# Linear attention with a gated FFN: o transposed tile by tile, output projection among the last Q groups, phi of Q on VectorE

## The chip, the core and the metric

The kernel runs on one core of a Trainium2 chip. The core has five engines, each with an instruction queue of its own that it works off in order: PE (TensorE, matrix products into PSUM), DVE (VectorE), ACT (ScalarE), POOL (GpSimd) and SP (SyncE, which only starts transfers). Sixteen DMA engines carry the transfers between HBM and SBUF. The metric is the device time of one execution in microseconds (us), the median of several runs.

## What is computed

Inputs are bf16: x is 2048 tokens of 1024, wqkv 1024 x 3072, wo 1024 x 1024, the FFN's weights 1024 x 3584 (gate, up) and 3584 x 1024 (down). The reference, cut to what matters:

```python
x = A_x
xn = _layernorm(x, axis=-1)
# _A_ref: 32 heads of 32
phi = lambda t: jnp.where(t > 0, t + 1, jnp.exp(t)) + 1e-6
pq, pk = phi(q), phi(k)
kv = jnp.einsum("bhsd,bhse->bhde", pk, v)
z = jnp.einsum("bhsd->bhd", pk)
num = jnp.einsum("bhqd,bhde->bhqe", pq, kv)
den = jnp.einsum("bhqd,bhd->bhq", pq, z)[..., None] + 1e-6
o = num / den
s = o @ wo                               # [2048, 1024]
# _B_ref
f = (_silu(xn @ w_gate) * (xn @ w_up)) @ w_down
return x + s * _silu(f)
```

## The kernel before

It has three stages. The first (lines 256 to 597) normalizes x, transposes it, computes K and V for 16 tiles of 128 tokens, and accumulates the sums of pk times v (kvz). It also computes the Q groups of tokens 0 to 1023 (pass 0). The second (lines 599 to 705) is where the change lies. The third is the FFN with the final sum.

Products with seven instead of eight blocks are used for Q and for the FFN. A Q group (class QGroup, line 205) is 256 columns of Q for 1024 tokens: seven products of four matmuls each (M3, M4, M1, M5, M2, N7, N6), in three parts. part_a computes M3 into PSUM tile X, ACT copies X to u (line 228), M4 goes into Y, and DVE adds Y to u (line 231). part_b adds M1 (tile Z) to u (line 236), accumulates M5 into X and M2 into Y, and ACT takes exp and relu of both (lines 186, 187). part_c accumulates N7 and N6, DVE subtracts them from u (line 246), and ACT takes exp and relu of that. part_d is phi: min(exp, 1) + eps, then + relu, two instructions (lines 190, 191) for each of the group's two rows of 128 columns x 1024 tokens. The buffers of exp and relu, e_t and r_t, come from a pool of three (phiw, line 195). In stage two the four groups of pass 1 run; row 0 of each has its phi on DVE, row 1 on POOL (line 674, and self.eng).

emit_KVZ (line 614) masks kvz into the matrix KVZ, on DVE. emit_ND (line 624) takes one tile of 128 tokens: eight matmuls of phi(q) with KVZ give numerator and denominator in three PSUM tiles (nd_ps, a pool of three banks, psA), DVE computes the reciprocal and writes o_sb (four buffers), and SP stores o_sb to o_dram in HBM. After the fourth tile of a block of 512 tokens, one DMA transpose reads the block of o_dram back as oT (line 652). Blocks 0 and 1 have tiles of their own; blocks 2 and 3 go into the space of wq_sb.

emit_S (line 654) is one unit of the output projection: eight matmuls of oT with wo into a PSUM bank (s_ps; the five banks of psB are shared with the Q groups), for one tile of 128 tokens and 512 of 1024 columns. ACT copies it to s_sb (two buffers), and after the second unit of a tile SP stores s_sb to s_dram (line 669). The FFN's last part reads s_dram.

Stage two has 16 ND tiles and 32 S units. Its order on PE, DVE, ACT and POOL is the written one (manual_schedule, line 672); SP's is not in that list, and its order is the scheduler's. Written are: the Q groups with one ND tile of block 0 in each, then all S units in order, with the ND tiles of blocks 1 to 3 between them, one for each S unit in block 1, one for every two after that. The FFN's first weights (load_w, line 174; a pair of 512 KB loads) take the buffers of phi(q) as these come free. sum_w (line 166) forms sums of weight blocks on DVE; the FFN's first groups need those of pair 0.

The order of waits is the same in both kernels: a transpose waits until its stores have landed, an S unit waits for its transpose, the o_sb of a tile waits until the store of the tile four before it has landed, and the matmuls of an ND tile wait until DVE has read the nd banks of the tile before.

Of the kernel before, what the change touches and what calls it, by code (L numbers as in the profile page):

```python
# [10 lines left out]
ALU = mybir.AluOpType  # L11
# [10 lines left out]
def kernel(  # L22
# [11 lines left out]
    nc = tc.nc  # L34
    P = 128
    x2 = A_x.flatten_outer_dims()
    out2 = out.flatten_outer_dims()
    S, D = x2.shape
# [8 lines left out]
    NB = S // TB  # L47
    TPB = TB // P
# [70 lines left out]
    def blk_rows(t_dram, b):  # L119
        return t_dram[b * TB:(b + 1) * TB, :]  # L120
# [65 lines left out]
        nc.scalar.activation(out=e, in_=t, func=ACT.Exp)  # L186
        nc.scalar.activation(out=r, in_=t, func=ACT.Relu)

    def emit_phi(eng, dst, e, r):
        eng.tensor_scalar(out=e, in0=e, scalar1=1.0, scalar2=EPS, op0=ALU.min, op1=ALU.add)  # L190
        return eng.tensor_tensor(out=dst, in0=e, in1=r, op=ALU.add)  # L191

    p12 = ExitStack()
    wqp = p12.enter_context(tc.tile_pool(name="wqp", bufs=1))
# [10 lines left out]
    class QGroup:  # L205


        def __init__(self, p, m, eng1):
            w = wq_sb[:, :, m * FW:(m + 1) * FW]
            self.lhs, self.rhs = block_operands(w, ws_all[:, m // 2, m % 2]), x_operands(p)  # L210
            self.eng = (nc.vector, eng1)
            self.out = wgu.tile([P, 2, SP_TOK], BF16, name="pqT", tag=("wg_sb" if m % 2 == 0 else "wu_sb"))
            pqT_tiles[(p, m)] = self.out
            self.row = {}
# [31 lines left out]
                nc.vector.tensor_tensor(out=r, in0=self.u[:], in1=acc[:], op=ALU.subtract)  # L246
                emit_exp_relu(e, r, r)

        def part_d(self):
            for i in range(2):  # L250
                emit_phi(self.eng[i], self.out[:, i, :], *(t[:] for t in self.row[i]))

    ET = mybir.EngineType
    FRONT_ORDER = {ET.PE, ET.DVE, ET.Activation, ET.Pool}
# [1 line left out]
    with ExitStack() as p1:  # L256
# [179 lines left out]
        def emit_B_out(i, c):  # L436
            kv_ps = kv_tiles.pop((i, c))
            if c < NCC:
                if c == 0:
                    er_tiles[i] = phi_tiles()  # L440
                emit_exp_relu(*(t[:, c * CW:(c + 1) * CW] for t in er_tiles[i]), kv_ps[:])
                if c == NCC - 1:
                    pk_tiles[i] = work.tile([P, D], BF16, name="pk_sb", tag="pk_sb")
                    emit_phi(nc.vector, pk_tiles[i][:], *(t[:] for t in er_tiles.pop(i)))
            else:
                vc = c - NCC
                nc.scalar.copy(out=v_of(i)[:, vc * GPC:(vc + 1) * GPC, 0:P],
                               in_=kv_ps[:].rearrange("p (g c) -> p g c", c=P))
# [50 lines left out]
        with tc.manual_schedule(engines=FRONT_ORDER):  # L499

            warm_up(14)
            emit_stats(0, parts=(0,))
            emit_stats(0, parts=(1,))
            emit_aggr(0)
            emit_stats(1, parts=(0,))
            emit_rstd_act(0)
            emit_T(0, lambda: emit_stats(1, parts=(1,)))
            warm_up(2)
            emit_B_mm(0, 0)
            emit_aggr(1)  # L510
# [36 lines left out]
            emit_C(0)  # L547
            emit_B_mm(2, 3)
            emit_B_out(1, 3)
            emit_N(TPB)  # L550
            emit_N(TPB + 1)
            emit_C(1)
            emit_B_mm(3, 0)
            emit_B_out(2, 3)
            emit_C(2)
            emit_B_out(3, 0)
            emit_B_mm(3, 1)
            emit_T(TPB)
            emit_B_out(3, 1)
            emit_N(TPB + 2)  # L560
            emit_N(TPB + 3)
            emit_B_mm(3, 2)
            emit_T(TPB + 1)
            emit_B_out(3, 2)
            emit_B(3, 3)
            fill(2)

            Q0 = 2 * TPB + 1
            qp0 = deque(range(NM_Q))
            for i in range(TPB, NT):  # L570
                grp = QGroup(0, qp0.popleft(), nc.vector) if i >= Q0 and (i - Q0) % 2 == 0 and qp0 else None
                nf = 1 if grp else 2
                emit_B(i, 0)
                fill(nf)
                emit_C(i - 1)
                if grp:
                    grp.part_a()
                emit_B(i, 1)
                fill(nf)
                if grp:  # L580
                    grp.part_b()
                if i == TPB:
                    emit_T(TPB + 2)
                emit_B(i, 2)
                fill(nf)
                if i == TPB:
                    emit_T(TPB + 3)
                if grp:
                    grp.part_c()
                emit_B(i, 3)  # L590
                if grp:
                    grp.part_d()
                fill(nf)
            emit_C(NT - 1)
            assert not later and not qp0
# [3 lines left out]
    with ExitStack() as p2:  # L599
# [5 lines left out]
        oT_cd = wq_sb[:].rearrange("p c n -> p (c n)").rearrange("p (b g t) -> p b g t", b=2, t=TB)  # L605
        s_tiles = {}
        wo_sb = wop.tile([P, G, D], BF16, name="wo_sb")
        for c in range(NCC):
            nc.sync.dma_start(out=wo_sb[:, :, c * CW:(c + 1) * CW], in_=wo_v[:, :, c * CW:(c + 1) * CW])

        def oT_of(b):
            return (oT_ab[:] if b < 2 else oT_cd)[:, b % 2]
# [11 lines left out]
        def emit_ND(b, t):  # L624
# [23 lines left out]
                    in1=rden[:, g0:g0 + ng, :, None].to_broadcast([P, ng, HPG, DH]),  # L648
                    op=ALU.mult)
            nc.sync.dma_start(out=o_dram[r0:r0 + P, :], in_=o_sb[:])  # L650
            if t == TPB - 1:
                nc.sync.dma_start_transpose(out=oT_of(b), in_=blk_rows(o_dram, b))

        def emit_S(b, t, cc):
            oT = oT_of(b)
            ttok = slice(t * P, (t + 1) * P)
            if (b, t) not in s_tiles:
                s_tiles[(b, t)] = work.tile([P, D], BF16, name="s_sb", tag="s_sb")
            s_sb = s_tiles[(b, t)]
            s_ps = psB.tile([P, CW], FP32, name="s_ps", tag="B")  # L660
            for c in range(G):
                mm = nc.tensor.matmul(s_ps[:], lhsT=oT[:, c, ttok], rhs=wo_sb[:, c, cc * CW:(cc + 1) * CW],  # L662
                                      start=(c == 0), stop=(c == G - 1))
                if c == 0:
                    marks[("S", b, t, cc)] = mm
            nc.scalar.copy(out=s_sb[:, cc * CW:(cc + 1) * CW], in_=s_ps[:])  # L666
            if cc == NCC - 1:
                r0 = b * TB + t * P
                nc.sync.dma_start(out=s_dram[r0:r0 + P, :], in_=s_tiles.pop((b, t))[:])

        PREF = 3
        with tc.manual_schedule(engines=FRONT_ORDER):

            qs = [QGroup(NPASS - 1, m, nc.gpsimd) for m in range(NM_Q)]
            qs[0].part_a()
            emit_KVZ()
            qs[0].part_b()
            emit_ND(0, 0)
            for m in range(1, NM_Q):
                qs[m].part_a()  # L680
                qs[m - 1].part_c()
                emit_ND(0, m)
                qs[m - 1].part_d()
                qs[m].part_b()
            qs[-1].part_c()
            qs[-1].part_d()
            nd = deque((b, t) for b in range(1, NB) for t in range(TPB))
            ns = 0
            for b in range(NB):
                for t in range(TPB):  # L690
                    for cc in range(NCC):
                        if nd and (nd[0][0] == 1 or ns % 2 == 0):
                            emit_ND(*nd.popleft())
                        emit_S(b, t, cc)
                        ns += 1
                    if (b, t) == (NB - 1, 0):
                        sum_w(0, 0)
                        sum_w(0, 1)
                if b == 0:
                    load_w(0, after=marks[("S", 0, TPB - 1, 0)])  # L700
                    load_w(1, after=marks[("S", 0, TPB - 1, 0)])
                if b == 1:
                    load_w(2, after=marks[("S", 1, TPB - 1, 0)])
    p12.close()
    ps12.close()

# [369 lines left out]
```

## Time and profile before

| | us |
|---|---|
| median of 3 runs | 783.53 (782.23 to 784.75) |
| the profiled execution | 783.54 |
| its span, first to last instruction | 781.7 |
| PE busy, share of the span | 754.5, 97% |
| DVE busy | 476.9, 61% |
| ACT busy | 276.2, 35% |
| POOL busy | 73.9, 9% |
| mean granted TensorE clock | 0.99 |

The span is 1.8 us shorter than the time, which also counts what lies around it. An engine's busy time is the sum of its instructions; the timeline lists instructions of one engine in order of time and joins neighbours of one kind. In brackets stands the idle time of the engine ahead of an instruction, and what ended it. The chain of waits gives PE 76% of the span; most of it is matmuls of Q and of the FFN, which all go through line 131.

### The profile page before, as it was taken

The numbers are of one execution on the slowest core, as the hardware profiler recorded it, in microseconds if no ns is written. First come the engines' busy times: TensorE is split into PE (matmuls) and PEld (weight loads), VectorE is DVE, ScalarE is ACT, GpSimd is POOL, SyncE is SP. The second block draws the span as 40 slices with busy tenths as digits, with TensorE's granted clock in tenths as the row PEclk, the third lists the DMA queues.
The fourth block names the chain that finished last, engine by engine and source line by source line (L and its number), as shares of the span: only waits on it lengthen the run. The fifth ranks groups of instructions, "written<-read, shape, count | busy, mean of one in ns | idle before, by whom it ended". The sixth has DMA issues, their size and how long they took to land.

```text
span 781.7 us, 9960 instructions
## 1 busy us (share of the span) xinstructions
PE 754.5 (97%) x3764; PEld 354.0 (45%) x3764; DVE 476.9 (61%) x892; ACT 276.2 (35%) x481; POOL 73.9 (9%) x118
## 2 busy tenths in 40 slices
PE   8999999985987999999999999999999999999997
PEld 3554444442443444444444444444444444444454
DVE  6686663374753066787767877676856554554454
ACT  4454555554322343333433433344334111111111
POOL 3311000035300000000000000000000122122220
PEclk9999999999999999999999999999999999999999
DMA  9607000043598243366543654433859964444300
GB/s 321 215 14 196 10 1 1 0 135 81 147 257 258 91 142 109 108 184 183 152 121 108 190 174 141 135 109 120 278 192 318 382 223 175 175 154 144 133 29 28
DMA packets 127279, 115.98 MB, mean 148 GB/s; under 512 B 29056, under 2 KB 108032, under 8 KB 125952
## 3 DMA queue, kind: packets, MB, share of 16 engines
q1 hardware_dynamic: 126944, 114.97, 46.1%
q8 instruction: 29, 0.48, 0.3%
q10 hardware_dynamic: 288, 0.39, 0.2%
q14 instruction: 18, 0.15, 0.1%
HBM read 70.52 MB, written 38.54 MB: 140 GB/s over the span
## 4 chain that ended last, share of the span: by engine, by line
PE 76%; issue 13%; DMA 4%; POOL 3%; DVE 2%; ACT 1%; SPq 0%; POOLq 0%; DVEq 0%
PE X L131 28%; PE Y L131 27%; PE Z L131 9%; PE kv_ps L430 5%; PE s_ps L662 4%; DMA wq_sb<-o_dram 2%; POOL e_t L190 1%; DMA o_dram<-o_sb 1%; DMA oT<-o_dram 1%; POOL pqT L191 1%; ACT e_t L186 1%; DMA xp<-in_A_x_dram 1%; DVE stats L323 1%; PE nd_ps L635 0%; PE tr_ps L398 0%
## 5 line engine op out<-in xcount | busy, mean ns | idle before, releaser
L131 PEld LDWEIGHTS <-ws_all 128*128 128x128 bf16 x1420 | 138.1, 98 | 175.1 <-issue 14.0
L741 DVE TENSOR_TENSOR q<-n,Y 128x512 f32<-128x512 f32 x63 | 43.3, 688 | 133.6 <-PE Y L131 133.6
L430 PE MATMUL kv_ps<-wkv_sb,xnT 128*128 128x512 bf16 x512 | 115.6, 379 | 0.5 <-DVE xnT L413 0.5
L131 PEld LDWEIGHTS <-xs 128*128 128x128 bf16 x616 | 58.0, 98 | 63.1
L1009 POOL TENSOR_TENSOR o_out<-y,xres 128x512 bf16<-128x512 f32 x28 | 34.0, 1215 | 522.6 <-DVE y L1008 522.6
L430 PEld LDWEIGHTS <-xnT 128*128 128x128 f16 x512 | 49.3, 98 | 57.0 <-DVE xnT L413 0.7
L131 PE MATMUL Y<-xs,ws_all 128*128 128x512 f16 (+3 forms) x308 | 70.3, 360 | 0.0
L131 PE MATMUL X<-xnT,ws_all 128*128 128x512 f16 (+1 forms) x280 | 70.2, 379 | 0.0
L131 PE MATMUL Z<-xs,ws_all 128*128 128x512 f16 x224 | 57.5, 379 | 0.0
L131 PE MATMUL Y<-xnT,ws_all 128*128 128x512 f16 x224 | 57.5, 379 | 0.0
L131 PE MATMUL X<-xs,ws_all 128*128 128x512 f16 x224 | 57.5, 379 | 0.0
L863 ACT ACTIVATE g<-cg 128x512 bf16<-128x512 f32 x56 | 35.3, 631 | 54.2 <-DVE cg L756 54.2
L747 DVE TENSOR_TENSOR u<-Z,q 128x512 f32<-128x512 f32 x63 | 43.2, 685 | 16.0 <-PE Z L131 15.9
L863 ACT ACTIVATE g<-X 128x512 bf16<-128x512 f32 x28 | 16.7, 597 | 100.0 <-PE X L131 100.0
L737 ACT COPY n<-X 128x512 f32<-128x512 f32 x63 | 36.9, 586 | 27.9 <-PE X L131 27.9
L888 DVE TENSOR_TENSOR ho<-g,up 128x1024 bf16<-128x1024 bf16 x56 | 38.1, 684 | 0.5
L666 ACT CAST s_sb<-s_ps 128x512 bf16<-128x512 f32 x32 | 18.6, 586 | 54.1 <-PE s_ps L662 43.7
L1008 DVE TENSOR_TENSOR y<-y,s_in 128x512 f32<-128x512 f32 x31 | 22.2, 716 | 21.1 <-ACT y L1002 15.8
L662 PE MATMUL s_ps<-wo_sb,wq_sb 128*128 128x512 bf16 x128 | 29.8, 395 | 5.4 <-DMA wq_sb<-o_dram 5.4
L131 PEld LDWEIGHTS <-wg_sb 128*128 128x128 bf16 x224 | 21.9, 98 | 26.4
L131 PEld LDWEIGHTS <-wu_sb 128*128 128x128 bf16 x224 | 21.9, 98 | 26.4
L662 PE MATMUL s_ps<-wo_sb,oT 128*128 128x512 bf16 x128 | 30.8, 393 | 1.5 <-DMA oT<-o_dram 1.5
(141 smaller groups left out, 1034.5 us busy)
## 6 DMA issues: line engine op xcount, KB each, us to landing
h_dram<-ho SPq DMA_DIRECT2D x56, 256.0 KB, 2.5
wg_sb<-in_B_w_gate_dram SPq DMA_DIRECT2D x14, 512.0 KB, 3.9
wu_sb<-in_B_w_up_dram SPq DMA_DIRECT2D x14, 512.0 KB, 4.0
wdr<-in_B_w_down_dram SPq DMA_DIRECT2D x14, 512.0 KB, 3.8
ws_all<-h_dram SPq DMA_DIRECT2D x4, 1792.0 KB, 7.5
wds_dram<-wdsA SPq DMA_DIRECT2D x14, 384.0 KB, 2.6
hp_a<-h_dram SPq DMA_DIRECT2D x3, 1792.0 KB, 7.4
o_dram<-o_sb SPq DMA_DIRECT2D x16, 256.0 KB, 2.4
```

What stands on the lines that cost most here:

```text
L131: marks["mm"] = nc.tensor.matmul(acc[:, 0:c1 - c0], lhsT=lhs(k), rhs=rhs(k)[:, c0:c1], start=(first and k == 0), stop=(k == n - 1), skip_g ...
L186: nc.scalar.activation(out=e, in_=t, func=ACT.Exp)
L430: mm = nc.tensor.matmul(kv_ps[:], lhsT=xn_tok_ap(i)[:, dc, :], rhs=wkv_sb[:, dc, c * CW:(c + 1) * CW], start=(dc == 0), stop=(dc == DC - 1))
L662: mm = nc.tensor.matmul(s_ps[:], lhsT=oT[:, c, ttok], rhs=wo_sb[:, c, cc * CW:(cc + 1) * CW], start=(c == 0), stop=(c == G - 1))
L666: nc.scalar.copy(out=s_sb[:, cc * CW:(cc + 1) * CW], in_=s_ps[:])
L737: nc.scalar.copy(out=n[:], in_=self.X[:])
L741: nc.vector.tensor_tensor(out=self.q[:], in0=n[:], in1=self.Y[:], op=ALU.add)
L747: nc.vector.tensor_tensor(out=self.u[:], in0=Z[:], in1=self.q[:], op=ALU.add)
L863: nc.scalar.activation(out=self.g[:, i, j * TB:(j + 1) * TB], in_=src, func=ACT.Silu)
L888: nc.vector.tensor_tensor(out=self.ho[:, i], in0=self.g[:, i], in1=self.up[:, i], op=ALU.mult)
L1008: nc.vector.tensor_tensor(out=t[:], in0=t[:], in1=self.s_in[:, i, cs], op=ALU.mult)
L1009: (nc.vector if last else nc.gpsimd).tensor_tensor(out=self.o_out[:, i, cs], in0=t[:], in1=self.xres[:, i, cs], op=ALU.add)
```

## The change

phi of Q is done by DVE for both rows, and part_d takes the row as an argument. In the Q groups of pass 0 nothing else changes. After every ND tile, SP issues the store of o_sb and, behind it, a transpose of that tile alone, 128 tokens. SP's instructions in stage two keep the written order. The stores of S are issued by ACT. KVZ is computed ahead of the first Q group's part_a. ND tiles stand at other places among the Q groups; from the third group on (m = 2) two S units stand in each group, four in all before the groups are done. After that an ND tile and an S unit alternate until the ND tiles are used up. The loads of weight pairs 0 to 2 follow, on SP's queue, the last ND tile of blocks 1 to 3, and the marks that held them back are gone. sum_w of pair 0 stands ahead of the last four S units.

```diff
-    def emit_phi(eng, dst, e, r):
-        eng.tensor_scalar(out=e, in0=e, scalar1=1.0, scalar2=EPS, op0=ALU.min, op1=ALU.add)
-        return eng.tensor_tensor(out=dst, in0=e, in1=r, op=ALU.add)
+    def emit_phi(dst, e, r):
+        nc.vector.tensor_scalar(out=e, in0=e, scalar1=1.0, scalar2=EPS, op0=ALU.min, op1=ALU.add)
+        nc.vector.tensor_tensor(out=dst, in0=e, in1=r, op=ALU.add)
...
-        def part_d(self):
-            for i in range(2):
-                emit_phi(self.eng[i], self.out[:, i, :], *(t[:] for t in self.row[i]))
+        def part_d(self, i):
+            emit_phi(self.out[:, i, :], *(t[:] for t in self.row[i]))
...
-            if t == TPB - 1:
-                nc.sync.dma_start_transpose(out=oT_of(b), in_=blk_rows(o_dram, b))
+            nc.sync.dma_start_transpose(out=oT_of(b)[:, :, t * P:(t + 1) * P], in_=o_dram[r0:r0 + P, :])
...
-                nc.sync.dma_start(out=s_dram[r0:r0 + P, :], in_=s_tiles.pop((b, t))[:])
+                nc.scalar.dma_start(out=s_dram[r0:r0 + P, :], in_=s_tiles.pop((b, t))[:])
...
-        with tc.manual_schedule(engines=FRONT_ORDER):
-
-            qs = [QGroup(NPASS - 1, m, nc.gpsimd) for m in range(NM_Q)]
+        units = deque((b, t, cc) for b in range(NB) for t in range(TPB) for cc in range(NCC))
+        nds = deque((b, t) for b in range(NB) for t in range(TPB))
+
+        def s_unit():
+            emit_S(*units.popleft())
+
+        def nd_tile():
+            if nds:
+                b, t = nds.popleft()
+                emit_ND(b, t)
+                if t == TPB - 1 and 1 <= b <= PREF:
+                    load_w(b - 1)
+
+        with tc.manual_schedule(engines=FRONT_ORDER | {ET.SP}):
+
+            qs = [QGroup(NPASS - 1, m) for m in range(NM_Q)]
+            for c in range(NCC):
+                nc.sync.dma_start(out=wo_sb[:, :, c * CW:(c + 1) * CW], in_=wo_v[:, :, c * CW:(c + 1) * CW])
+            emit_KVZ()
             qs[0].part_a()
-            emit_KVZ()
             qs[0].part_b()
-            emit_ND(0, 0)
-            for m in range(1, NM_Q):
+            nd_tile()
+            qs[1].part_a()
+            qs[0].part_c()
+            qs[0].part_d(0)
+            nd_tile()
+            qs[1].part_b()
+            qs[0].part_d(1)
+            nd_tile()
+            qs[1].part_c()
+            qs[1].part_d(0)
+            for m in range(2, NM_Q):
                 qs[m].part_a()
-                qs[m - 1].part_c()
-                emit_ND(0, m)
-                qs[m - 1].part_d()
+                qs[m - 1].part_d(1)
                 qs[m].part_b()
-            qs[-1].part_c()
-            qs[-1].part_d()
-            nd = deque((b, t) for b in range(1, NB) for t in range(TPB))
-            ns = 0
-            for b in range(NB):
-                for t in range(TPB):
-                    for cc in range(NCC):
-                        if nd and (nd[0][0] == 1 or ns % 2 == 0):
-                            emit_ND(*nd.popleft())
-                        emit_S(b, t, cc)
-                        ns += 1
-                    if (b, t) == (NB - 1, 0):
-                        sum_w(0, 0)
-                        sum_w(0, 1)
-                if b == 0:
-                    load_w(0, after=marks[("S", 0, TPB - 1, 0)])
-                    load_w(1, after=marks[("S", 0, TPB - 1, 0)])
-                if b == 1:
-                    load_w(2, after=marks[("S", 1, TPB - 1, 0)])
+                nd_tile()
+                s_unit()
+                qs[m].part_c()
+                qs[m].part_d(0)
+                s_unit()
+            qs[-1].part_d(1)
+            while units:
+                nd_tile()
+                if len(units) == 2 * NCC:
+                    sum_w(0, 0)
+                    sum_w(0, 1)
+                s_unit()
```

More of the change, by code (lines that the diff above doesn't have):

```diff
@@ L205, with __init__ @@
     class QGroup:
-        def __init__(self, p, m, eng1):
+        def __init__(self, p, m):
             w = wq_sb[:, :, m * FW:(m + 1) * FW]
             self.lhs, self.rhs = block_operands(w, ws_all[:, m // 2, m % 2]), x_operands(p)
-            self.eng = (nc.vector, eng1)
             self.out = wgu.tile([P, 2, SP_TOK], BF16, name="pqT", tag=("wg_sb" if m % 2 == 0 else "wu_sb"))
@@ L443, in emit_B_out @@
                     pk_tiles[i] = work.tile([P, D], BF16, name="pk_sb", tag="pk_sb")
-                    emit_phi(nc.vector, pk_tiles[i][:], *(t[:] for t in er_tiles.pop(i)))
+                    emit_phi(pk_tiles[i][:], *(t[:] for t in er_tiles.pop(i)))
             else:
@@ L570 @@
             for i in range(TPB, NT):
-                grp = QGroup(0, qp0.popleft(), nc.vector) if i >= Q0 and (i - Q0) % 2 == 0 and qp0 else None
+                grp = QGroup(0, qp0.popleft()) if i >= Q0 and (i - Q0) % 2 == 0 and qp0 else None
                 nf = 1 if grp else 2
@@ L591 @@
                 if grp:
-                    grp.part_d()
+                    grp.part_d(0)
+                    grp.part_d(1)
                 fill(nf)
@@ L607 @@
         wo_sb = wop.tile([P, G, D], BF16, name="wo_sb")
-        for c in range(NCC):
-            nc.sync.dma_start(out=wo_sb[:, :, c * CW:(c + 1) * CW], in_=wo_v[:, :, c * CW:(c + 1) * CW])
         def oT_of(b):
```

## The prediction

> **What bounds the kernel now.** I read the table of busy time by slice first: PE is at 9 tenths in 34 of 40 slices, so a change pays only where PE stands still or runs at a lower clock.
>
> ```profile
> PE   8999999985987999999999999999999999999997
> ```
>
> The low digits in the middle (8, 5, 9, 8, 7) are slices of 19.5 us from 156 to 254 us. Next came PE's own timeline, in order of time, from the last Q groups to the first FFN matmul (start us, us, what, in brackets the idle time before it and its releaser):
>
> ```profile
> 171.59 1.86 PE L131 MATMUL qY<-xs,ws_all 128*128 128x512 f16 x4 [3.14 <-ACT r_t L187]
> ...
> 182.33 1.02 PE L131 MATMUL qY<-xs,ws_all 128*128 128x512 f16 x4 [2.46 <-ACT r_t L187]
> ...
> 193.07 1.86 PE L131 MATMUL qY<-xs,ws_all 128*128 128x512 f16 x4 [4.44 <-ACT r_t L187]
> ...
> 215.83 3.63 PE L662 MATMUL s_ps<-wo_sb,oT 128*128 128x512 bf16 x16 [1.45 <-DMA oT<-o_dram]
> ...
> 235.26 3.63 PE L662 MATMUL s_ps<-wo_sb,wq_sb 128*128 128x512 bf16 x16 [1.70 <-DMA wq_sb<-o_dram]
> ...
> 253.45 15.64 PE L662 MATMUL s_ps<-wo_sb,wq_sb 128*128 128x512 bf16 x64 [3.74 <-DMA wq_sb<-o_dram]
> ```
>
> With two more gaps (1.20 and 1.26) these idle times make 19.4 us. The stage runs from 153.93 (first Q matmul) to 268.94 (first FFN matmul): 115.0 us. Its matmuls alone, from start-to-start times in this timeline (four of Q or FFN 0.865, eight nd 0.47, eight s_ps 1.73): 4 groups x 7 x 0.865 = 24.2, 16 x 0.47 = 7.5, 32 x 1.73 = 55.3, the last kvz 0.3: 87.3 us. So 27.7 us are there to be had, no more: 19.4 of gaps, and most of the other 8.3 is clock, as stretches of the span show (granted clock, DMA share and GB/s stand last):
>
> ```profile
> 171.60:175.40 3.80, 3.80 (x17) 1.91 (x17) 3.06 (x8) 2.38 (x5) 0.07 (x1) 0.56 0.00 0
> 175.40:178.00 2.60, 2.60 (x14) 1.19 (x13) 2.50 (x6) 1.52 (x3) 2.60 (x1) 1.00 0.27 101
> 193.00:199.00 6.00, 5.93 (x22) 2.67 (x22) 3.65 (x10) 2.43 (x5) 2.45 (x1) 0.52 0.24 55
> ```
>
> After gaps of 3.14 and 4.44 us the clock is near half for some 4 us; after 2.46 it is not. The list of waits tells who is behind the first gaps: ACT, named there, waits for buffers that POOL holds (us in total, times, longest).
>
> ```profile
> ACT e_t L186 <- POOL pqT L191: 12.4, 3, 4.4
> PE s_ps L662 <- DMA wq_sb<-o_dram: 5.4, 2, 3.7
> ```
>
> POOL's phi takes 3.63 + 2.12 = 5.75 us a row; there are three e/r tiles. The later gaps are the four block transposes. SP's timeline:
>
> ```profile
> 188.77 4.00 SPq L652 DMA_TRANSPOSE oT<-o_dram  x1
> ...
> 209.04 4.65 SPq L652 DMA_TRANSPOSE oT<-o_dram  x1
> 213.74 0.58 SPq L669 DMA_DIRECT2D s_dram<-s_sb  x1
> ...
> 247.51 3.79 SPq L652 DMA_TRANSPOSE wq_sb<-o_dram  x1
> ```
>
> A transpose of 1 MB holds SP about 3.9 us and lands after 6.0 (5.9 to 6.7).
>
> **The change, part by part.**
>
> *Phi on VectorE.* POOL's four pairs go; VectorE gets four more at 1.15 us (165.44 to 166.62 is one pair). The POOL gaps go. What is late next: VectorE, nearly full. I walk the Q stage with this profile's steps: qu, r_t 0.60 each, a phi pair 1.15, the three rden, reciprocal and o_sb of a tile (ND) 2.0; on ACT a pair from PSUM 0.97, from r_t 1.2, qu's copy 0.58. ND(0,1) ends at 166.6, u 167.2, phi 168.35, ND(0,2) 170.35. Only then comes group 1's r_t (171.0), which frees the PSUM bank of group 2's Z: PE waits 0.8. ACT makes group 1's four activations, 171.05 to 173.45, then group 2's copy of X (174.05), for which M5 waits: 2.15. ND(0,2) waits 0.65 for nd banks. Group 3 finds its operands ready. KVZ, now written ahead of group 0, costs nothing: before and after, VectorE waits for qY at 156.39 and has u ready before nd at 158.7. In all 3.6 us where 11.2 were (3.14 + 2.46 + 1.20 + 4.44): the stage's 33.7 us of PE work (four groups, five ND, four S units) and 0.3 end at 191.4.
>
> *S units among the Q groups* cost their 1.73 each wherever they stand; they fill PE while VectorE works. S(0,0) wants its o at 176.3: o_sb at 161.3, landed by 165.4 (4.1 in that window), transposed by 169. wo, issued at 155.6, lands in 8.8 at most. The loop then alternates ND and a unit; the old loop's step is 2.32 (199.40, 201.72, 204.04) against 2.20 of matmuls: 11 x 0.12 = 1.4 us.
>
> *Transposes by tile, SP in written order.* Each tile now puts on SP: store, a wait until it has landed, transpose. Behind that wait stand the next store and the weight loads; for the store waits VectorE (o_sb has four buffers), and for VectorE PE's nd banks. The price of a store is in the DMA issues of narrow windows (us to landing last):
>
> ```profile
> o_dram<-o_sb SPq DMA_DIRECT2D x1, 256.0 KB, 2.0
> ...
> o_dram<-o_sb SPq DMA_DIRECT2D x1, 256.0 KB, 2.6
> ...
> o_dram<-o_sb SPq DMA_DIRECT2D x1, 256.0 KB, 6.0
> ```
>
> 2.0 is with idle queues, 2.6 just behind a transpose (233.2), 6.0 behind weight loads (222.1). No row has a transpose of 128 tokens. Bounds of its hold on SP: 0.33, the shortest plain issue, and 3.8, that of the whole block. Data flow during a transpose decides:
>
> ```profile
> 188.80:189.80 1.00, 0.00 (x0) 0.00 (x0) 0.69 (x1) 0.00 (x0) 0.92 (x2) 1.00 0.00 0
> 189.80:190.80 1.00, 0.00 (x0) 0.00 (x0) 0.00 (x0) 0.00 (x0) 1.00 (x1) 1.00 0.70 121
> 190.80:191.80 1.00, 0.00 (x0) 0.00 (x0) 0.00 (x0) 0.00 (x0) 1.00 (x1) 1.00 1.22 269
> ```
>
> Nothing for 1 us, then 269 to 290 GB/s for as long as SP is held. Plain issues hold 0.33 to 0.45 us whether they carry 256 KB or 1 MB; so the rest of the 3.9 grows with the data: 0.35 + 3.5/4 = 1.2, landing 1.8 after that. A step of SP is then 2.6 + 1.2 + 0.1 = 3.9 us against 2.32 of the loop, and SP falls behind. Counting tiles 0 to 15: group 3's last phi leaves VectorE at 192.75, so tile 5 is written by 194.8; its store lands at 196.9, its transpose is issued by 198.2; tile 6 202.1, tile 7 206.0. Two weight issues take 1.0; store 8 lands at 213.0. VectorE wants that buffer for tile 12 at 208.9 (the loop's eighth ND, 191.4 + 7 x 2.32, and 1.25 to its first write, as from 198.93 to 200.18), so it waits 4.1, and for 13, 14, 15 until 216.9, 220.8, 224.7. Tile 14's writes free PE's nd banks, so the last ND ends at 222.3 instead of 215.2 (191.4 + 10 x 2.32 + 0.6): 7.1 us. The remaining 18 units (31.1) end at 253.4. Tile 15: weights and store 12 to 233.0, then three steps and T, landed at 247.8, wanted at 249.9. Hidden, with 2.1 us to spare. The third weight pair follows on SP at 246; at the slowest landing of such a load here (9.3) it is there at 256, and the FFN takes it up two weight steps of some 24 us later.
>
> The clock: the gap at tile 12 is about 3.6 us, so PE would run at half for some 4 us; the next steps leave 1.7 us each, which takes that in. It counts nothing; uncovered, 1.7. The Trainium skill, "TensorE: Matmul & The Clock Gate", section "What's actually happening", has the half clock after an idle window of about 3.4 us that runs free; by it the 3.14 us gap above need not have slowed, and did.
>
> The Trainium skill, "DMA: Bandwidth & Descriptors", section "Anatomy of one DMA", speaks against cutting transfers: about 2.0 us fixed each, then bytes at 436 GB/s. A 256 KB piece would be 2.6 us (an estimate from that page). Here only SP's hold repeats; were it 2.6, the step would be 5.3 and the time 780.7.
>
> *S stores on ACT.* SP loses 16 issues; ACT gets 16 of 0.40 to 0.45 (its two x loads at the start). Per two units ACT has 2 x 0.59 + 0.45 in 3.46: hidden; without cover 0.45 each. *sum_w* now follows the last ND on VectorE, 226 to 231; the FFN wants it at 255.
>
> Sum: 153.9 + 87.3 + 3.6 + 1.4 + 7.1 = 253.3 against 268.94. The FFN is untouched. 783.54 (the profiled run, span 781.7) - 15.5 = 768.0; the median, 783.53, is the same.
>
> **The rivals.**
> 1. Forecast: SP's step about 3.9; 762 to 775. Chance 0.62.
> 2. SP never binds: hold 0.33, weights no hindrance. For: the small hold of plain issues. Against: 6.0 behind weights. The end is 253.3 - 7.1 = 246.2, so 760.8. Chance 0.15.
> 3. A step of about 4.8 (hold 2.1, or more queueing, for which the DMA share of 0.93 around 216 to 236 speaks): from 188.4, where tile 4 is written, 12 steps, 8.8 for two weight pairs (1.0 of issue and 6.0 less 2.6, each), 1.8 of landing and 3.5 for the last tile: 260.1, so 774.7 to 780. Chance 0.11.
> 4. Slower: the transpose's hold does not shrink with its size (3.8). Against: the data flow above. The step is 6.5, the end 188.4 + 78 + 14.1 = 280.5, so 795. It decides from a hold of 2.8 (a step of 5.5), where the end is 268.9. Chance 0.12.
>
> **How the numbers follow.** The time is the first case's, 768.0. Low 759 takes in rival 2 with a cheaper Q stage; high 781 takes in rival 3; outside is rival 4. Faster by over 0.3% (about what three runs can tell) takes rivals 1 to 3: 0.86; within 0.3%, a hold near 2.8: 0.03; slower 0.11.
>
> **What would show it.** No POOL phi and no PE gap named ACT r_t over 2.5 us; transposes holding SP 1.0 to 1.5 us; VectorE's o_sb waiting for o_dram stores at tiles 12 to 15; the first FFN matmul near 253. Wrong if the hold is over 2 us, if stores land in over 3.5 us outside the weight loads, or if VectorE stretches the Q stage past 195.

## The result, and the profile after

The changed kernel took 777.07 us (median of 6 runs, 775.6 to 780.1) against 783.36 for the kernel before on the same chip (6 runs): ratio 0.9925, 95% interval 0.9902 to 0.9948. It is 6.3 us faster where 15.5 were forecast. The direction held and the time lies inside the range given; the size did not hold. The profiled execution took 777.21, its span 775.4.

PE's busy time by slice of the changed kernel, to be laid beside the line of before:

```profile
PE   8999999989969999999999999999999999999997
```

Before, four slices between 156 and 254 us were below 9 (8, 5, 8 and 7, with a 9 among them). Now there are two: the first, still at 8, and a lower one (6) at 213 to 233 us. PE's timeline of the changed kernel (start us, us, what, in brackets the idle time before it and what ended it):

```profile
174.19 1.05 PE L131 MATMUL qX<-xnT,ws_all 128*128 128x512 f16 x4 [2.69 <-ACT qu L227]
175.05 1.90 PE L131 MATMUL qY<-xnT,ws_all 128*128 128x512 f16 x4
...
220.17 1.20 PE L632 MATMUL nd_ps<-KVZ,pqT 128*128 128x132 bf16 x8 [6.37 <-DVE o_sb L642]
221.16 3.62 PE L658 MATMUL s_ps<-wo_sb,oT 128*128 128x512 bf16 x8
...
227.94 1.09 PE L632 MATMUL nd_ps<-KVZ,pqT 128*128 128x132 bf16 x8 [0.19 <-DVE o_sb L642]
...
247.12 3.63 PE L658 MATMUL s_ps<-wo_sb,wq_sb 128*128 128x512 bf16 x16 [0.83 <-DMA wq_sb<-o_dram]
...
259.38 3.63 PE L658 MATMUL s_ps<-wo_sb,wq_sb 128*128 128x512 bf16 x16 [0.50 <-DMA wq_sb<-o_dram]
262.84 1.03 PE L131 MATMUL X<-xs,wg_sb 128*128 128x512 f16 x4
```

The gaps named ACT r_t are gone. The first FFN matmul comes at 262.84 instead of 268.94, 6.1 us earlier, which is nearly the whole gain of 6.3. Of the stage's own time PE loses 2.69 us before M5 of group 2 (the third group), 6.37 before ND tile 13, and then waits at each of the last four tiles for its transpose (0.83, 0.50, 0.38, 0.50): the last S units start when their transposes land. So the end of the stage is set by the last transpose. The chain of waits that ended last says the same: from 204.98 us, where store 7 is issued, to 259.38 it runs through the landings of stores 7 to 15 and of the last transpose, which make 41.0 of these 54.4 us. SP's timeline of the changed kernel shows how it came to be so late:

```profile
203.69 1.23 SPq L648 DMA_TRANSPOSE oT<-o_dram  x1
204.98 0.58 SPq L647 DMA_DIRECT2D o_dram<-o_sb  x1
210.34 1.23 SPq L648 DMA_TRANSPOSE oT<-o_dram  x1
211.63 0.57 SPq L177 DMA_DIRECT2D wg_sb<-in_B_w_gate_dram  x1
212.29 0.53 SPq L179 DMA_DIRECT2D wu_sb<-in_B_w_up_dram  x1
212.88 1.59 SPq L647 DMA_DIRECT2D o_dram<-o_sb  x1
219.48 1.23 SPq L648 DMA_TRANSPOSE wq_sb<-o_dram  x1
...
234.80 2.34 SPq L647 DMA_DIRECT2D o_dram<-o_sb  x1
242.98 1.24 SPq L648 DMA_TRANSPOSE wq_sb<-o_dram  x1
...
255.76 1.29 SPq L648 DMA_TRANSPOSE wq_sb<-o_dram  x1
```

A transpose of 128 tokens holds SP 1.23 to 1.30 us, as worked out (1.2). Longer than worked out is the time from a store's issue to its transpose: 5.36 us for store 7 (204.98 to 210.34), 6.60 for store 8 behind the first weight pair, 8.18 for store 12 behind the second. The DMA issues of narrow windows give the same as landing times (stores 6, 7, 8, 12, us last):

```profile
o_dram<-o_sb SPq DMA_DIRECT2D x1, 256.0 KB, 3.5
...
o_dram<-o_sb SPq DMA_DIRECT2D x1, 256.0 KB, 5.3
...
o_dram<-o_sb SPq DMA_DIRECT2D x1, 256.0 KB, 6.6
...
o_dram<-o_sb SPq DMA_DIRECT2D x1, 256.0 KB, 8.2
```

The list of waits (us in total, times, longest) has both ends of the chain: VectorE waits for the store that holds its buffer, and SP stands 44.5 us in front of its 16 transposes.

```profile
DVE o_sb L642 <- DMA o_dram<-o_sb: 13.0, 5, 6.9
...
SPq L648 <- DMA o_dram<-o_sb: 44.5, 16, 5.8
```

Is it bandwidth that SP waits for? Two stretches of the span (length, busy us of PE, PEld, DVE, ACT, POOL, then granted clock, DMA share, GB/s):

```profile
194.00:229.00 35.00, 26.94 (x158) 13.20 (x159) 22.33 (x73) 6.33 (x11) 0.00 (x0) 0.85 0.55 158
229.00:263.00 34.00, 31.63 (x143) 13.77 (x144) 8.47 (x21) 9.96 (x17) 0.00 (x0) 1.00 0.75 208
```

In the first of them the DMA engines are busy 55% of the time. The rest of the time they are idle, and SP, which has the next work for them, stands in front of a transpose for 44.5 us in all; the runs with another order on SP show below that the two belong together.

### The profile page after: what moved, and what is told of

Read it like the earlier page. It is cut to its first block, busy times and chain, and to the rows that moved or that the text cites. A ratio compares the mean times of both kernels' runs of the same rounds, so it can differ in the third digit from the quotient of the medians.

```text
span 775.4 us, 9920 instructions
## 1 busy us (share of the span) xinstructions
PE 752.6 (97%) x3724; PEld 353.3 (46%) x3764; DVE 482.5 (62%) x900; ACT 276.3 (36%) x481; POOL 50.9 (7%) x110
## 4 chain that ended last, share of the span: by engine, by line
PE 87%; DMA 7%; DVE 4%; ACT 1%; issue 1%; SPq 1%; DVEq 0%
PE X L131 28%; PE Y L131 28%; PE kv_ps L428 13%; PE Z L131 9%; DMA o_dram<-o_sb 5%; PE qX L131 2%; PE qY L131 2%; PE s_ps L658 2%; DVE o_sb L642 1%; PE kvz L456 1%; PE qZ L131 1%; PE nd_ps L632 1%; DMA xp<-in_A_x_dram 1%; SPq L648 0%; ACT e_t L186 0%
## 5 line engine op out<-in xcount | busy, mean ns | idle before, releaser
L428 PE MATMUL kv_ps<-wkv_sb,xnT 128*128 128x512 bf16 x497 | 113.9, 379 | 1.0 <-DVE xnT L411 0.5
```

What stands on the lines that cost most here:

```text
L428: mm = nc.tensor.matmul(kv_ps[:], lhsT=xn_tok_ap(i)[:, dc, :], rhs=wkv_sb[:, dc, c * CW:(c + 1) * CW], start=(dc == 0), stop=(dc == DC - 1))
```

## The experiments

Each run was timed against the kernel before on the same chip (its median was 782.9 to 783.4 us on each). "First FFN" is the start of the first FFN matmul in the profiled execution, whose time is 514.4 to 515.6 us more than that, except in the run with late weights (521.8).

| kernel | us | ratio, 95% interval | first FFN |
|---|---|---|---|
| before | 783.53 | | 268.9 |
| changed | 777.07 | 0.9925 [0.9902, 0.9948] | 262.8 |
| changed, again | 777.21 | 0.9914 [0.9883, 0.9945] | 262.8 |
| transpose behind the next store | 771.83 | 0.9866 [0.9845, 0.9887] | 256.7 |
| same, and pair 1's sums later | 765.84 | 0.9779 [0.9759, 0.9799] | 249.4 |
| five o_sb buffers | 772.22 | 0.9867 [0.9846, 0.9889] | 257.1 |
| weight pairs last | 775.03 | 0.9901 [0.9879, 0.9924] | 254.2 |
| weight pairs on ACT's queue | 773.96 | 0.9881 [0.9864, 0.9897] | 259.5 |
| SP's order from the scheduler | 769.75 | 0.9833 [0.9819, 0.9848] | 255.6 |
| block transposes | 784.42 | 1.0022 [1.0008, 1.0036] | 270.2 |
| phi alone, on the kernel before | 777.58 | 0.9931 [0.9910, 0.9951] | 262.6 |
| S stores on SP | 794.19 | 1.0133 [1.0104, 1.0162] | 280.2 |
| phi of row 1 on POOL again | 773.35 | 0.9883 [0.9851, 0.9914] | 259.0 |
| phi on POOL, order and sums | 761.61 | 0.9737 [0.9713, 0.9761] | 246.3 |

### Is what the profile shows systematic?

The changed kernel was profiled a second time, unaltered.

> The changed kernel unaltered, a second profile of it. Theory A (the steps of SP as measured are systematic): 776 to 778 us, transposes of tiles 7 and 8 issued at 209 to 211 and 218 to 220, a wait of VectorE for o_dram stores near 6 us at tile 12. Theory C (an instruction fetch of 16 KB that happened to meet store 7, and a half clock that happened to follow the 2.69 us gap, are chance): store 7 lands in 2.6 to 3.5 us, its transpose is issued near 206, the wait at tile 12 is near 4 us, and the profiled execution's time is 772 to 775.

It took 777.21 us (5 runs, 771.82 to 778.26). Store 7 landed in 3.0 us this time and its transpose was issued at 207.93 instead of 210.34, but store 8 took 7.5 and store 12 9.5 where the first profile had 6.6 and 8.2, and the last transpose went out at 255.74, as before. PE's wait at ND tile 13 was 6.41, its half clock after the 2.69 us gap was there again. So the late landing of store 7 was not there every time; the late end was. The gain at store 7 was lost again at the two weight pairs.

### SP's order: the transpose behind the next tile's store

If SP's chain of store, landing and transpose is what costs, one store put ahead should hide the landing behind it.

```diff
-            nc.sync.dma_start_transpose(out=oT_of(b)[:, :, t * P:(t + 1) * P], in_=o_dram[r0:r0 + P, :])
...
                 emit_ND(b, t)
+                stored.append((b, t))
+                if len(stored) > 1 or not nds:
+                    emit_T_o(*stored.popleft())
+                if not nds:
+                    emit_T_o(*stored.popleft())
```

> The transpose of a tile is issued behind the store of the next tile, so SP no longer stands still until a store has landed. Theory A (SP's order sets the end: store, wait for its landing, transpose, tile after tile, with the weight pairs between): SP's work for a tile falls from 3.9 to 9 us to some 1.8 us (0.5 + 1.25), under the loop's 2.32; no o_sb waits for a store beyond 1 us; the first FFN matmul starts at 248 to 251 instead of 262.8, the time is 763 to 766 us. Theory B (the DMA engines are full in this stage, so stores and transposes land late in whatever order they are issued): the first FFN matmul stays at 258 or later, the time over 772 us.

771.83 us, 5.2 us better than the changed kernel, but short of the 763 to 766. The waits for transposes at the tail were gone (S units run from 229.1 to 256.7 without one). A new wait had come ahead of them. On VectorE, in this run:

```profile
222.20 0.42 DVE L152 TENSOR_TENSOR ws_all<-wg_sb 128x512 bf16<-128x512 bf16 x1 [7.22 <-DMA wg_sb<-in_B_w_gate_dram]
```

and so on PE:

```profile
223.15 1.20 PE L632 MATMUL nd_ps<-KVZ,pqT 128*128 128x132 bf16 x8 [7.04 <-DVE o_sb L642]
```

The sums of weight pair 1, which belong to the FFN's loop, had been scheduled on VectorE ahead of the last ND's o_sb, and stood there for 7.22 us until their weights were loaded. In the changed kernel they already stand behind the last o_sb (239.89 us against 232.22), so moving them alone had nothing to win there. The next run keeps the new order of SP and writes these sums behind the last ND:

```diff
                     sum_w(0, 0)
                     sum_w(0, 1)
+                    sum_w(1, 0)
+                    sum_w(1, 1)
...
-                if p == 0 and m + 1 < NM:
+                if p == 0 and 0 < m < NM - 1:
```

> The transpose of a tile behind the store of the next tile, as in the run before, and in addition both weight sums of pair 1 written behind the last ND on VectorE, so that VectorE's last o_sb cannot stand behind a weight load (7.22 us there). Theory A (SP's chain of store, landing, transpose was what the tail lost, and the 7 us wait is what hid it in the first try): PE's wait of 7.04 before its last ND goes, last ND near 216 to 218, S units without a wait, first FFN matmul 248 to 251, 763 to 766 us. Theory B (the DMA engines' load at the weight pairs sets the end, whoever waits): the wait moves to another place and the time stays at 771 to 773.

765.84 us, first FFN matmul at 249.37, in the range of theory A. The last ND starts at 217.69, PE's waits from ND(1,1) on are 0.49 and 0.16, and the clock is 1.00 from 194 us on. The first of the two stretches shown above, in this run:

```profile
194.00:229.00 35.00, 33.90 (x204) 16.89 (x207) 30.66 (x94) 8.16 (x15) 0.00 (x0) 1.00 0.96 237
```

The DMA share is 0.96, where the changed kernel had 0.55: transfers almost without pauses. A single store behind a weight pair still lands late here (store 8, 7.8 us), but the transpose of tile 7 and store 9 go out while it lands, and VectorE waits for stores only twice, 0.9 us in all, where it waited 13.0. Theory B, that the DMA engines' load sets the end, falls.

### Who makes the stores late: five buffers, the weights' place, the weights' queue

Five o_sb buffers instead of four:

```diff
-            o_sb = work.tile([P, D], BF16, name="o_sb", tag="o_sb", bufs=4)
+            o_sb = work.tile([P, D], BF16, name="o_sb", tag="o_sb", bufs=5)
```

> o_sb gets five buffers instead of four. Theory A (SP's chain sets the end, and VectorE's waits for o_sb buffers are only its echo): the waits move from tile 11 on to tile 12 on, the transposes are issued at the same times, the first FFN matmul stays at 262 to 263.5, the time within 1.5 us of 777. Theory C (as the prediction had it, the o_sb buffers set the end, since the last ND tile comes late and 18 units follow): the last ND tile comes one SP step earlier, the first FFN matmul at 258 to 259.5, the time some 4 us lower, 773.

772.22 us, near the number of theory C (its first FFN matmul, 257.1, is earlier than the 258 to 259.5 expected). The profile does not bear out its mechanism alone: VectorE still waits 3.86, 1.39 and 1.53 us for stores, now from tile 13 on, the last transposes are still waited for (2.13 and 0.46), and SP's 5.5 us lead at T15 (250.31 against 255.76) stands at 2.1 by T5, where PE had no half clock after the 2.69 us gap, and at 4.1 by T7, whose store landed in 3.4 us. The four runs lie at 770.98 to 773.07, the eleven of the changed kernel at 771.82 and 775.6 to 780.1, so the gain itself is real; how much of it is the buffer stays open.

All three weight pairs behind the last transpose:

```diff
-                if t == TPB - 1 and 1 <= b <= PREF:
-                    load_w(b - 1)
+                if not nds:
+                    for m in range(PREF):
+                        load_w(m)
```

> The three weight pairs are issued behind the last transpose. Theory A: the two pairs that stood between the tiles cost SP 1.3 us of issue and some 4.5 us of later landing each, 11.6 us in all; the last transpose lands near 248 instead of 259.3, the S units end at 250 to 254, and the FFN then waits up to 4 us for pair 0 and its sums: time 768 to 772. Theory B (DMA engines full, order indifferent): the last transpose lands after 255, and the late weights come on top: time 777 or more.

775.03 us. The part about SP came true: the last transpose was issued at 245.18 instead of 255.76, and S units ran from 226.6 to 254.2 without a wait, so the pairs do cost SP's chain some 10 us. The FFN then paid for it. PE in this run:

```profile
254.22 1.03 PE L131 MATMUL X<-xs,wg_sb 128*128 128x512 f16 x4
...
261.95 1.86 PE L131 MATMUL X<-xnT,ws_all 128*128 128x512 f16 x4 [4.72 <-ACT n L749]
```

ACT, which has n to copy, is behind the last S stores, and those shared the DMA engines with 3 MB of weights (ACT stands idle 6.12 and 4.49 us there; the profile names the landing of weights for the first, of an S store for the second). The FFN starts 8.6 us earlier than in the changed kernel, and takes 7.4 us longer from there.

The pairs 0 and 1 issued by ACT, at nearly the same places of the program, to tell SP's own queue from the engines that all queues share:

```diff
+        eng = nc.scalar if m < 2 else nc.sync
-        d1 = nc.sync.dma_start(out=wg_sb[:], in_=wg_v[:, :, cols])
+        d1 = eng.dma_start(out=wg_sb[:], in_=wg_v[:, :, cols])
```

> The changed kernel with the weight loads of the pairs 0 and 1 issued by ACT, in ACT's written order, and not by SP; the same bytes at nearly the same places of the program. Theory A (a store behind a pair lands late because it stands behind 2 MB in SP's own queues): stores 8 and 12 land in 2.6 to 4 us and not in 6.6 and 8.2, SP saves the four issues too, the last transpose is issued 5 to 9 us earlier than 255.8, first FFN matmul 254 to 258, 768 to 772 us. Theory B (the DMA engines are full of the weights, whichever queue they come from): the stores land in 6 to 8 us as before, 775 to 778 us.

773.96 us, between the two. Stores that followed ACT's weights landed nearly as late as behind SP's (stores 6 and 8 of this run, from the DMA issues of narrow windows):

```profile
o_dram<-o_sb SPq DMA_DIRECT2D x1, 256.0 KB, 5.4
...
o_dram<-o_sb SPq DMA_DIRECT2D x1, 256.0 KB, 6.5
```

So a store is late because of the load on the engines that all queues share (a pair is 1 MB, not the 2 MB of the expectation), not because of SP's own queue: theory B is right on the landing. What was won (last transpose 5.9 us earlier) goes with ACT having issued both pairs by 211.6 us, 22 us before SP got to the second (233.44), so that store 12 met no weights and landed in 3.0 us.

### The written order of SP

Without SP in the list, the scheduler sets its order:

```diff
-        with tc.manual_schedule(engines=FRONT_ORDER | {ET.SP}):
+        with tc.manual_schedule(engines=FRONT_ORDER):
```

> The changed kernel with SP's queue out of the written order: the scheduler sets it. It puts one store ahead of some transposes (two stores, then two transposes, from tile 6 on) and pulls the weight pairs apart. Theory A (each store's landing in SP's in-order chain is what costs): pairs of stores wait for one landing in place of two, the last transpose is issued some 3 to 8 us earlier, 769 to 774 us. Rival (the written order is worth something): 778 to 782 us.

769.75 us: the written order of SP costs 7.3 us against the scheduler's. SP's wait in front of transposes fell from 44.5 us in 16 to

```profile
SPq L648 <- DMA o_dram<-o_sb: 24.6, 11, 3.7
```

and the waits of the last S units are gone. From tile 6 on two stores share one wait; the two loads of a weight pair also stand apart, the first already at 196.89 us. Which of the two brought how much the run can't tell.

### What the other parts are worth

Block transposes in the changed kernel, as before (one of 512 tokens behind the fourth store):

```diff
-            nc.sync.dma_start_transpose(out=oT_of(b)[:, :, t * P:(t + 1) * P], in_=o_dram[r0:r0 + P, :])
+            if t == TPB - 1:
+                nc.sync.dma_start_transpose(out=oT_of(b), in_=blk_rows(o_dram, b))
```

> The transposes are by block of 512 tokens again, all else as in the changed kernel. Theory A: SP's chain is short again (0.5 us a store), but an S unit waits for its whole block: some 10 us at the first unit among the Q groups, where o of the fourth tile is stored at 180 and the transpose takes 6 us, and some 6 us at block 1; the first FFN matmul at 264 to 268, the time 778 to 783. A rival that has the gain come from phi on VectorE and from the S units' places alone, and nothing from the tiles: first FFN matmul at 261 or earlier, time under 776.

784.42 us, no faster than before. PE in this run:

```profile
187.42 0.61 PE L659 MATMUL s_ps<-wo_sb,oT 128*128 128x512 bf16 x1 [10.15 <-DMA oT<-o_dram]
...
222.00 1.89 PE L659 MATMUL s_ps<-wo_sb,oT 128*128 128x512 bf16 x4 [6.26 <-DMA oT<-o_dram]
```

S units among the Q groups have nothing to work on until a whole block is stored. The tile-wise transposes are worth 7.3 us, and the rest of the change is worth nothing without them: phi alone, in the kernel before, brings 5.6 us (below), and here all of that is lost.

The S stores back on SP's queue, in the written order:

```diff
-                nc.scalar.dma_start(out=s_dram[r0:r0 + P, :], in_=s_tiles.pop((b, t))[:])
+                nc.sync.dma_start(out=s_dram[r0:r0 + P, :], in_=s_tiles.pop((b, t))[:])
```

> The changed kernel with the S stores back on SP's queue. Theory A (SP's step sets the end): each S store adds an issue of 0.4 to 0.6 us and now waits on SP for ACT's copy, steps grow by 0.3 to 0.5 us a tile, last transpose 4 to 7 us later, 780 to 785 us. Rival (SP's slack takes it in, the S stores on ACT were worth nothing): 776 to 778.

794.19 us, 17 us worse than the changed kernel, far beyond what was expected. PE in this run:

```profile
242.56 5.57 PE L658 MATMUL s_ps<-wo_sb,wq_sb 128*128 128x512 bf16 x16 [7.37 <-ACT s_sb L662]
252.74 0.84 PE L658 MATMUL s_ps<-wo_sb,wq_sb 128*128 128x512 bf16 x3 [4.61 <-ACT s_sb L662]
...
262.33 18.01 PE L658 MATMUL s_ps<-wo_sb,wq_sb 128*128 128x512 bf16 x71 [4.30 <-ACT s_sb L662]
```

It is not 16 issues of 0.4 us. The store of an S tile stands behind transposes of later tiles, which wait for their stores; s_sb has two buffers, so ACT waits for the store (12.13, 9.11 and 8.52 us), the PSUM banks stay full, and PE stops.

phi of row 1 on VectorE, alone, in the kernel before:

```diff
-            qs = [QGroup(NPASS - 1, m, nc.gpsimd) for m in range(NM_Q)]
+            qs = [QGroup(NPASS - 1, m, nc.vector) for m in range(NM_Q)]
```

> The kernel before with one part of the change alone: phi of row 1 of the Q groups of pass 1 on VectorE. Theory A (the Q stage gains and the block transposes take it back, since they leave SP as late as before): PE's gaps named ACT r_t over 2.5 us go, the Q stage ends 5 to 8 us earlier, the waits for oT and wq_sb transposes grow from 6.9 to 11 to 14 in sum, 779 to 783 us. Rival (the Q stage's gain stands): 773 to 776.

777.58 us, between both. The last Q matmuls start at 181.12 instead of 193.07, a gain of 12 us, more than expected. PE in this run:

```profile
188.35 0.61 PE L662 MATMUL s_ps<-wo_sb,oT 128*128 128x512 bf16 x1 [5.74 <-DMA oT<-o_dram]
...
228.10 3.63 PE L662 MATMUL s_ps<-wo_sb,wq_sb 128*128 128x512 bf16 x15 [1.71 <-DMA wq_sb<-o_dram]
...
246.28 16.53 PE L662 MATMUL s_ps<-wo_sb,wq_sb 128*128 128x512 bf16 x63 [3.72 <-DMA wq_sb<-o_dram]
```

With one more of 0.75 the waits for block transposes make 11.9 us instead of 6.9. This part alone brings as much as the whole change.

The other way round, the changed kernel with that part undone:

```diff
-            emit_phi(self.out[:, i, :], *(t[:] for t in self.row[i]))
+            emit_phi(self.out[:, i, :], *(t[:] for t in self.row[i]), eng=nc.gpsimd if i == 1 and self.p else nc.vector)
```

> The changed kernel with one part undone: phi of row 1 of the Q groups of pass 1 is back on POOL (two operations of 3.6 and 2.1 us a row). Theory A (the Q stage and SP's chain add up, the chain being the later limit): the Q stage ends some 4 to 8 us later than the 193.2 of the changed kernel, the tail is as late or up to 6 us later, 778 to 783 us. Rival (SP's chain alone sets the end, and the Q stage's gain is lost in it): 776 to 778 us.

773.35 us (771.11 to 777.29): below the ranges of both theories, 3.7 us faster than the changed kernel, though the intervals of the two ratios overlap. The profile says why. POOL keeps up now: with S units in the groups it stands idle 1.4 to 4.1 us ahead of each phi after its first. VectorE has the chain that M5 waits for. In the changed kernel a phi pair (group 0's row 1) stands on VectorE ahead of group 1's r_t:

```profile
167.35 0.42 DVE L190 TENSOR_SCALAR e_t<-e_t 128x1024 bf16<-128x1024 bf16 x1
167.87 0.69 DVE L191 TENSOR_TENSOR pqT<-e_t,r_t 128x1024 bf16<-128x1024 bf16 x1
...
170.49 0.68 DVE L245 TENSOR_TENSOR r_t<-qu,qX 128x512 bf16<-128x512 f32 x1
```

and with phi on POOL that r_t starts at 169.03, and PE's wait is shorter and keeps its full clock:

```profile
172.74 1.02 PE L131 MATMUL qX<-xnT,ws_all 128*128 128x512 f16 x4 [1.56 <-ACT qu L229]
```

ND(1,1), tile 5, comes at 190.08 instead of 193.19. Of these 3.1 us, 1.1 are the shorter wait, 1.7 the clock behind it (from M5 to ND(1,1) it takes 17.34 us against 19.00), and 0.3 were there before the wait. They go through SP's chain to the end, as its first late tile is written that much earlier.

### The best version: phi on POOL, order and sums

The edits of three runs together: the transpose behind the next store, pair 1's sums behind the last ND, and phi of row 1 on POOL, as in their diffs above.

> Three edits of the earlier runs together: the transpose of a tile behind the next tile's store, both weight sums of pair 1 behind the last ND, and phi of row 1 of the Q groups of pass 1 back on POOL. Theory A (with S units among the Q groups VectorE is the late engine there, so phi of Q on VectorE costs PE about 3 us in the Q stage, and with SP's chain out of the way that reaches the end): ND(1,1) near 190, first FFN matmul near 246, 761 to 764 us. Rival (the better time with phi on POOL was SP's chain meeting other transfers, not the Q stage): 765 to 767 us, as with phi on VectorE.

761.61 us (5 runs, 761.3 to 764.73), 15.5 us faster than the changed kernel and 21.7 faster than the one before. ND(1,1) is at 190.24, the first FFN matmul at 246.34, and PE has one wait over 0.5 us in the stage. Two stretches of it:

```profile
194.00:229.00 35.00, 34.38 (x207) 17.00 (x205) 27.30 (x82) 8.39 (x15) 2.28 (x2) 1.00 1.03 250
229.00:246.00 17.00, 16.95 (x79) 7.59 (x78) 0.00 (x0) 4.48 (x9) 0.00 (x0) 1.00 0.96 260
```

Against the version with phi on VectorE it gains 4.2 us. The two intervals just touch (0.9761 and 0.9759), but together with the run before and both profiles theory A stands; as there, 1.7 us of the gain are the clock, half in one profile and full in the other.

## Why the prediction was right in kind and wrong in size

The step that failed is the price of SP's steps. The prediction put a store's landing at 2.6 us, and at 6.0 behind weights; stores 6 and 7 took 3.5 and 5.3, stores 8 and 12, behind weights, 6.6 and 8.2. By tile 15 the transposes were 11.1 us late, and what was to be hidden stood in the way. Otherwise the mechanism was the one forecast: POOL's gaps go, SP's serial steps become the limit, VectorE's o_sb waits for stores at tiles 12 to 15 (6.89, 1.40, 1.06 and 2.61 us), PE waits behind it. By its own steps:

- The bound of 27.7 us to be had was good: the best version takes 22.6 of them (268.94 to 246.34).
- The transpose's hold on SP (1.2 us, read from the data flow of the block's transpose) was 1.23 to 1.30, though its row for plain issues was read too narrowly: in the profile before they hold 0.33 to 0.58 us, and up to 4.05 behind weight loads, not 0.33 to 0.45. The transpose's landing was 3.1 us after issue at the quietest (median 3.3) against the 3.0 put in. The loop's pace of 2.32 us was met. Rival 4, the one on the other side, fell with the hold. (Two sums are off by little: the gain adds up to 15.6, not 15.5, and the end at which rival 4 decides to 268.5, not 268.9.)
- The Q stage, forecast to end at 191.4, ended at 193.19. The wait before M5 was 2.69 instead of 2.15, and the 0.8 ahead of it did not come; but the 4.1 us after it ran at a clock of 0.62, which loses 1.6. The prediction had counted no half clock in this stage. (Its row for the gap of 4.44 us has 0.52 over 6.0 us, longer than the "some 4 us" of the text.)
- SP's steps: the table follows the issue of the transposes, in the first profile.

| transpose of tile | forecast | measured | late by |
|---|---|---|---|
| 5 | 198.2 | 198.89 | 0.7 |
| 7 | 206.0 | 210.34 | 4.3 |
| 8, behind pair 0 | 213.0 | 219.48 | 6.5 |
| 11 | 224.7 | 232.14 | 7.4 |
| 12, behind pair 1 | 233.0 | 242.98 | 10.0 |
| 15 | 244.7 | 255.76 | 11.1 |

Of the 11.1 us, 0.7 come from the Q stage; 3.7 from stores 6 and 7 (landing in 3.5 and 5.3 us instead of 2.6, of which store 7's lateness was not there in the second profile, which lost it again at the pairs); 2.1 at pair 0, of which 1.3 is a slip in the working, where the transpose's own hold was left out between 206.0 and 213.0, and the rest store 8's 6.6 instead of 6.0 and the weights' issues; 1.0 at store 11; 2.5 at pair 1, mostly store 12's 8.2 instead of 6.0; and 1.1 in the last three steps, of 4.65, 4.15 and 3.98 us instead of 3.9. Landings of over 3.5 us outside the weight loads were the prediction's own second sign of being wrong.

- That the last transpose is "Hidden, with 2.1 us to spare" (landed at 247.8) was the sentence that cost most. It landed in time for 259.38, 11.6 us later; less the 2.1 to spare, that is the 9.5 us by which the first FFN matmul missed 253.3. The same term showed on both paths: the last ND tile, which the sum has end at 222.3 by way of VectorE's buffers, ended at about 228.9, and the other 3 us came at the tail, mostly as the waits of the last four tiles (2.2). Two limits lay 2.1 us apart, and one of them was a sum of sixteen serial waits, each priced at its quiet value. Over the ten steps from tile 5 an error of 0.2 us a step would have used that up.
- The landing behind weights was taken from one row (6.0). The two profiles of the changed kernel have 6.6 to 9.5. The Trainium skill, "DMA: Bandwidth & Descriptors", section "Anatomy of one DMA", gives a fixed 2.0 us and then the bytes at 436 GB/s, a fit for transfers that GpSimd issues; for 256 KB that would be 2.6 us (an estimate from that page). The stores here, which SP issues, met that only with little else moving (2.0 to 2.6), and 3.3 to 3.6 were common with S stores and transposes about.
- That ACT hides the issues of the S stores was right (PE has no wait for s_sb in the changed kernel); what the same stores would do on SP in written order (17 us) was not worked out, so the prediction did not see that the rest of the change depends on this part.
- phi on VectorE was given the credit for the Q stage. It has it only in the old order (5.6 us alone); among S units POOL keeps up, and the part costs 3 to 4 us (3.7 and 4.2 by the medians, 3.3 both times by the ratios). The prediction had the price in its working, 3.6 us of waits of PE behind a late VectorE, but never compared it with leaving phi where it was.
- That SP's written order itself costs (7.3 us against the scheduler's, 11.2 against the order with one store ahead and the sums moved) was not among the rivals: each started from the order as written and asked only how long a step is.

Not settled: what share of the fifth buffer's gain is the buffer's. The S units' new place was not run by itself with tile-wise transposes in the old order.

## What to carry to other kernels

A queue that waits for its own store before the next transfer turns each landing into a serial step; here the DMA engines were busy 0.55 of 35 us with it and 0.96 of the same stretch without. One more store ahead of the wait, with two sums moved out of the way, was worth 11.2 us here, more than the whole change had brought. Price such a chain by the landings under load, not the quiet ones, and where a serial chain is "hidden with a little to spare", let the error of a step times the number of steps decide whether it is. When a wait on one engine disappears by two edits at once, ask which of them did it: here either alone did, and with the S units in place phi on VectorE only moved work to the engine that had become late.

## What the runs showed of the hardware

The clock after the same gap differs between executions. Ten profiled executions have the wait of 2.69 us before M5 of group 2; in seven the granted clock from 172 to 178 us is 0.72 to 0.76, in three it is 1.00, with the same instructions on PE around it (both profiles of the unaltered kernel are among the seven). The two with a gap of 1.56 us have 1.00. The Trainium skill, "TensorE: Matmul & The Clock Gate", section "What's actually happening", ties the half clock to an idle window of about 3.4 us that runs free. A position of the window that differs from run to run fits what is seen; its length does not, since 2.69 us can't hold such a window. The measurement decides here: the clock fell after a shorter gap than the page gives.

Store 7's landing of 5.3 us in the first profile: the DMA view of that moment (206 to 210 us; queue, packets, MB, share) has one packet of an instruction load, 16 KB,

```profile
q8 instruction: 1, 0.02, 2.5%
```

which took 1.61 us, from 207.26 to 208.87. The store's packets were through by 207.9, except for its last seven, which followed one behind another from 208.86 to 209.81 us; from 207.9 to 208.8 nothing else moved. In the second profile a packet like it passed at another moment (from 207.98, 0.93 us) and the store landed in 3.0 us. That the packet sat on the same engine as the store's last ones and made the store late is read from their times alone; it was not tried.
